# Query weights of a decode kernel: one load over 128 partitions, or four loads over strided partitions

## The chip, the cores and the metric

The kernel runs on one core of one Trainium2 chip. The metric is the device time in microseconds (us). Before the change it is 1275.88 us, the median of three runs (1275.86 to 1275.93). The core has TensorE (matrix products), VectorE, ScalarE and GpSimd, a sequencer called SyncE or SP that here only issues transfers, and 16 DMA engines that carry data between HBM and the on-chip memory SBUF, which has 128 partitions.

## The reference, cut to what matters

One token goes through a layer norm, and the result through an attention block with a long cache (16 query heads, 8 key/value heads, 65,536 positions of 256 values, bf16) and through a gated feed-forward block. The two are added to the input.

```python
B, Sq, D = 1, 1, 448
Hq, Hkv, Sk, Dh = 16, 8, 65536, 256
...
def _A_ref(x, k_cache, v_cache, wq, wo):
    ...
    q = (x @ wq).reshape(B, Sq, Hq, Dh).transpose(0, 2, 1, 3)
    scores = jnp.einsum("bhqd,bhkd->bhqk", q, k) * (Dh ** -0.5)
    p = _softmax(scores, axis=-1)
    o = jnp.einsum("bhqk,bhkd->bhqd", p, v)
    return o.transpose(0, 2, 1, 3).reshape(B, Sq, Hq * Dh) @ wo
...
x = A_x
xn = _layernorm(x, axis=-1)
return x + _A_ref(xn, A_k_cache, A_v_cache, A_wq, A_wo) + _B_ref(xn, B_w_r, B_w_gate, B_w_up, B_w_down)
```

The query weights `wq` are 448 x 4096 values, 3584 KB. The keys and the values are 256 MB each. Every byte is used once.

## The kernel before

**Tiling.** A key/value head's cache is cut into four units (`U` = 4): in each, every one of the 128 partitions holds 128 positions of 256 values (`SBN` = 128 positions, 64 KB for a partition, 8 MB for a unit). There are 32 units of K and 32 of V. They go through `ring`, an SBUF area of three slots (line 92): K units use slots 0 and 1 in turn, V units slot 2, and the last V units slots 0 and 1 too. Slot 2 first holds the query weights (`wq_area`, line 96: 14,336 values, 28 KB, in each partition) and small temporaries of the layer norm.

**Work on a unit.** TensorE transposes K in pieces of 128 x 128 (`k_T`), VectorE and ScalarE copy the transposed pieces to `kt_all`, TensorE multiplies them with the current queries (`k_QK`) and brings the scores back to 128 partitions (`k_JT`). After the four units of a head come the maximum, the exponentials and the products with V (`pe_V`). One turn (`turn_K`) works on K of unit u and V of unit u - 4.

**Queues.** The program is written as lists of entries, one list for each engine, with waits by name (`W`), operations (`O`) and transfers. `item` (line 243) puts a transfer on SP's list: first its waits, then for each part of the item a DMA start that adds 16 to the semaphore of the part when the part has landed. `items[key]` keeps the semaphore and the count that stand for "all parts landed", and `W_item` makes an engine wait for that count. SP works through its list strictly in order; `emit` writes out the entries, and every DMA is started at line 949. The list begins with `wq`, which waits for nothing, then the K units 0 to 3 (units 0 to 4 in two halves each, with semaphores of their own), V unit 0, then K and V in turn (lines 291 to 300). K unit u waits until TensorE has done with unit u - 2, V unit t until V unit t - 1 is done with, and V unit 0 until the queries exist. Two tiny loads (the input and a weight row) are issued by ScalarE's queue.

**Who uses wq.** `pe_setup` makes TensorE wait for it (`W_item("pe", "wq")`) ahead of `qrow`, 28 products that give the query row. VectorE scales the row, four small products transpose it, and the queries go to `qT_sb`. The semaphore `wq` is used once more at the end, for a part of the last V unit (`LAST_SEMS`, line 16); counts for that continue from the total so far (`semtot`).

`flat_src` (line 266) sees a weight matrix in HBM as 128 rows of equal length, one for each partition:

```python
def flat_src(src, n):
    return src.rearrange("a b -> (a b)").rearrange("(p n) -> p n", p=P)
```

## Time and profile before

| | |
|---|---|
| median of three runs | 1275.88 us |
| the profiled execution | 1275.78 us |
| its span in the trace | 1274.5 us |
| HBM read | 549.03 MB, 431 GB/s over the span |
| busy: TensorE / VectorE / ScalarE / GpSimd | 952.7 / 571.6 / 436.8 / 8.1 us |
| the transfer of wq | 3584 KB, 11.5 us from issue to landing |

The span is what the trace covers, from the first to the last recorded event of the execution; the device time holds about 1.3 us more. Times in the views below are microseconds from the start of the span. A packet is one row of a transfer on one DMA engine; packets of under 512 bytes are mostly the semaphore writes at the end of a transfer, one on each engine. In a window of the DMA view, a packet belongs to the window in which it starts and brings its whole time with it, so that a short window's share can exceed 100%. In the chain of waits, a DMA piece is one transfer from its issue to its landing, or the part of it that nothing else covers.

### The profile page before, as it was taken

What the parts mean: (1) busy time and instruction counts of PE and PEld (TensorE: products, weight loads), DVE (VectorE), ACT (ScalarE), POOL (GpSimd) and SP (SyncE); (2) the same over time, 40 slices, a digit from 0 to 9 for tenths busy, and PEclk for the clock granted to TensorE, in tenths of its full rate; (3) what the DMA queues carried; (4) which work ended last, traced back from release to release, by engine and by line L of the source; (5) the groups of instructions that cost most, each with busy time, mean ns of one, the idle gap of its engine ahead of it and who ended that gap; (6) DMA issues with size and microseconds to landing.
All of it is one profiled execution on the core that took longest, in us unless ns stands there. A gap on an engine that the chain in (4) does not pass through costs nothing.

```text
span 1274.5 us, 23452 instructions
## 1 busy us (share of the span) xinstructions
PE 952.7 (75%) x9685; PEld 620.7 (49%) x9685; DVE 571.6 (45%) x1083; ACT 436.8 (34%) x656; POOL 8.1 (1%) x38
## 2 busy tenths in 40 slices
PE   4998987768767778677678677687776787776664
PEld 2776655445544455454455444454444554444321
DVE  4665544445434355344454343453444544434310
ACT  1554433244323334233333242343333333323300
POOL 2000000000000000000000000000000000000000
PEclk8999998899888899888898888998888998888886
DMA  9999999999999999999999999999999999999998
GB/s 406 431 433 436 436 436 428 434 430 442 434 432 428 436 430 440 434 432 428 436 432 438 434 432 428 436 434 438 432 432 432 432 438 434 436 428 434 427 433 365
DMA packets 12356, 549.18 MB, mean 431 GB/s; under 512 B 1335, under 2 KB 1978, under 8 KB 2874
## 3 DMA queue, kind: packets, MB, share of 16 engines
q1 hardware_dynamic: 12340, 549.03, 99.8%
q8 instruction: 7, 0.11, 0.0%
q14 instruction: 3, 0.02, 0.0%
q10 hardware_dynamic: 6, 0.00, 0.0%
HBM read 549.03 MB, written 0.00 MB: 431 GB/s over the span
## 4 chain that ended last, share of the span: by engine, by line
DMA 78%; PE 18%; ACT 2%; issue 1%; DVE 1%; SPq 0%; ACTq 0%; DVEq 0%
DMA ring<-in_A_v_cache_dram 69%; PE ps_o L428 13%; DMA ring<-in_A_k_cache_dram 5%; PE ps_t L428 3%; DMA kt_all<-in_A_wo_dram 2%; DMA ring<-in_A_wo_dram 2%; PE ps_q L428 2%; ACT kt_all L492 2%; PE ps_m L428 1%; SPq L949 0%; DVE kt_all L490 0%; ACT S_sb L573 0%; PE ps_s L428 0%; DVE kt_all L731 0%; DVE kt_all L854 0%
## 5 line engine op out<-in xcount | busy, mean ns | idle before, releaser
L428 PE MATMUL ps_t<-ident_f,ring 128*128 128x128 f32 x4096 | 585.2, 285 | 81.3 <-DMA ring<-in_A_k_cache_dram 59.6
L490 DVE COPY kt_all<-ps_t 128x1024 bf16<-128x1024 bf16 x768 | 486.7, 684 | 289.1 <-PE ps_q L428 284.9
L428 PEld LDWEIGHTS ps_t<-ident_f,ring 128*128 128x128 f32 x4096 | 448.7, 143 | 233.6 <-issue 133.8
L492 ACT ACTIVATE kt_all<-ps_t 128x1024 bf16<-128x1024 bf16 x256 | 262.2, 1024 | 498.0 <-PE ps_q L428 497.9
L428 PE MATMUL ps_o<-ring,p_sb 128*4 128x512 bf16 x2040 | 177.9, 511 | 206.1 <-DMA ring<-in_A_v_cache_dram 201.7
L428 PEld LDWEIGHTS ps_o<-ring,p_sb 128*4 128x4 bf16 x2040 | 53.5, 102 | 294.6 <-issue 267.5
L428 PE MATMUL ps_q<-kt_all,q_cur 128*2 128x512 bf16 x2056 | 164.5, 397 | 0.3 <-DVE kt_all L490 0.3
L514 ACT ACTIVATE s<-ps_q 98x512 bf16<-98x512 f32 x257 | 151.8, 591 | 1.3 <-PE ps_q L428 1.3
L596 DVE RECIPROCAL rs<-ps_m 128x4 f32<-128x4 f32 x29 | 5.3, 182 | 275.1 <-PE ps_m L428 275.1
L583 ACT ACTIVATE p_sb<-S_sb 128x128 bf16<-128x128 bf16 x64 | 18.9, 307 | 265.4 <-PE ps_o L428 262.6
L428 PEld LDWEIGHTS ps_s<-sel_bf,s 128*128 128x128 bf16 x1032 | 64.3, 97 | 5.2 <-ACT s L514 1.9
L428 PE MATMUL ps_s<-sel_bf,s 128*128 128x8 bf16 x1032 | 63.4, 167 | 1.3 <-ACT s L514 1.3
L639 DVE CAST ob_sb<-ps_o 100x512 bf16<-100x512 f32 x29 | 20.1, 692 | 90.9 <-PE ps_o L428 90.9
L428 PEld LDWEIGHTS ps_q<-kt_all,q_cur 128*2 128x2 bf16 x2056 | 26.3, 79 | 44.9 <-issue 44.9
L428 PEld LDWEIGHTS ps_m<-rowsum,ones_f 128*128 128x128 f32 x58 | 12.3, 265 | 21.9 <-issue 21.9
L492 ACT ACT_TABLE_LOAD x7 | 9.0, 1283 | 27.0 <-PE ps_q L428 27.0
L543 DVE TENSOR_REDUCE m1p<-S_sb (+1 forms) x33 | 13.9, 421 | 4.4
L428 PE MATMUL ps_m<-rowsum,ones_f 128*128 128x4 f32 x58 | 14.8, 326 | 0.0
L541 DVE CAST S_sb<-ps_s 128x256 f32 (+1 forms) x33 | 13.6, 413 | 1.9 <-PE ps_s L428 1.9
L573 ACT ACTIVATE S_sb<-S_sb,negmax 128x512 bf16<-128x512 bf16 x16 | 13.2, 852 | 3.3 <-DVE negmax L567 3.3
L428 PE MATMUL ps_m<-diag,ones_f 2*128 2x2 f32 x58 | 11.2, 260 | 3.7 <-DVE diag L558 0.6
L428 PEld LDWEIGHTS ps_m<-diag,ones_f 2*128 2x128 f32 x58 | 8.7, 187 | 10.6 <-DVE diag L558 10.6
(97 smaller groups left out, 125.4 us busy)
## 6 DMA issues: line engine op xcount, KB each, us to landing
ring<-in_A_k_cache_dram SPq DMA_DIRECT2D x10, 4096.0 KB, 28.3
ring<-in_A_v_cache_dram SPq DMA_DIRECT2D x1, 4096.0 KB, 23.1
ring<-in_A_wq_dram SPq DMA_DIRECT2D x1, 3584.0 KB, 11.5
ring<-in_A_wo_dram SPq DMA_DIRECT2D x1, 2688.0 KB, 28.5
ring<-in_A_v_cache_dram SPq DMA_DIRECT2D x1, 2048.0 KB, 27.2
ring<-in_B_w_gate_dram SPq DMA_DIRECT2D x1, 1568.0 KB, 17.1
ring<-in_B_w_up_dram SPq DMA_DIRECT2D x1, 1568.0 KB, 20.5
ring<-in_B_w_down_dram SPq DMA_DIRECT2D x1, 1568.0 KB
```

The source lines that it names most:

```text
L428: return pe.matmul(*a, **k)
L490: O(e, ("EV", s, m), lambda it: nc.vector.tensor_copy(out=kt[:, :], in_=tb[:, :]), f"ev{m}")
L492: O(e, ("EV", s, m), lambda it: nc.scalar.activation(out=kt[:, :], in_=tb[:, :], func=ACTF.Copy), f"ev{m}")
L514: O("act", ("EVQ", s), lambda it: nc.scalar.activation(out=s2[s % 2][0:QROWS, :], in_=ps_q[0:QROWS, :], func=ACTF.Copy), "evq")
L541: O("dve", ("SCOPY", u), lambda it: nc.vector.tensor_copy(out=S_sb[:, at(it, SBN), :], in_=ps_sn), "sc")
L543: O("dve", ("SMAX", u), lambda it: nc.vector.tensor_reduce(out=m1p[:, :, at(it, 1)], in_=S_sb[:, at(it, SBN), :].rearrange("p n i -> p i n ...
L573: O("act", ("EXP", h, i), lambda it, i=i: nc.scalar.activation(out=S_sb[:, :, i], in_=S_sb[:, :, i], func=ACTF.Exp, bias=negmax[:, i:i + 1 ...
L583: O("act", ("PC", t, c), lambda it: nc.scalar.activation(out=p_sb[:, c, :, :], in_=S_sb[:, n:n + CH, :], func=ACTF.Copy), "pc")
L596: O("dve", ("RS", t), lambda it: nc.vector.reciprocal(out=rs[:, :, :], in_=ps_m[0:P, C_TOT:C_TOT + NH * rep]))
L639: O("dve", ("OB", t), lambda it: nc.vector.tensor_copy(out=ob_sb[0:OROWS, :], in_=ps_o[0:OROWS, :]))
```

## The change

The transfer of `wq`, one over partitions 0 to 127, becomes four, still on SP's queue and still first in it. Each takes every n-th partition from partition o on, and the same rows of the weights in HBM:

```diff
-    item("wq", [(wq_area, flat_src(A_wq, WQN), "wq")])
+    item("wq", [(wq_area[o:P:n, :], flat_src(A_wq, WQN)[o:P:n, :], "wq") for o, n in ((0, 8), (4, 8), (2, 4), (1, 2))])
     for u in range(U):
         k_item(u)
     v_item(0)
```

| transfer | partitions | rows |
|---|---|---|
| (0, 8) | 0, 8, 16, ... 120 | 16 |
| (4, 8) | 4, 12, 20, ... 124 | 16 |
| (2, 4) | 2, 6, 10, ... 126 | 32 |
| (1, 2) | 1, 3, 5, ... 127 | 64 |

Together they cover each partition once. Every row is 28 KB as before. The count that stands for "wq has landed" becomes 64 in place of 16. On the engines' lists nothing else differs: the other four are the same, and SP's has four wq transfers of 16, 16, 32 and 64 rows where it had one of 128.

## The prediction

> **What bounds the kernel now.** I read the profile in this order: the page for the bound, the chain of waits for what starts and ends the run, the DMA packets in short windows for the first load, and the timeline of TensorE for who waits for it.

> From the page, in its order: the span, the DMA engines' busy share and rate in forty slices, the SP queue's packets, megabytes and share of 16 engines, and the chain by engine.

> ```profile
> span 1274.5 us, 23452 instructions
> ...
> DMA  9999999999999999999999999999999999999998
> GB/s 406 431 433 436 436 436 428 434 430 442 434 432 428 436 430 440 434 432 428 436 432 438 434 432 428 436 434 438 432 432 432 432 438 434 436 428 434 427 433 365
> ...
> q1 hardware_dynamic: 12340, 549.03, 99.8%
> ...
> DMA 78%; PE 18%; ACT 2%; issue 1%; DVE 1%; SPq 0%; ACTq 0%; DVEq 0%
> ```

> The run is one stream of 549.03 MB, and its 16 DMA engines are busy 99.8% of the span. No slice has a hole. So a microsecond more of transfer at the front has no gap behind it in which to vanish, and a microsecond less is a microsecond won. The chain's first pieces (start, length, what) show where the front lies:

> ```profile
> 0.74 0.39 SPq L949
> 1.13 0.06 issue
> 1.19 20.78 DMA ring<-in_A_k_cache_dram
> 21.96 0.04 issue
> 22.01 1.97 PE ps_t L428 x8
> ```

> SP issues the query weights (wq) at 0.74 for 0.39 us, then the first half of K unit 0 at 1.19; that half lands at 21.97, behind wq on the same engines, and only then does TensorE start on K. TensorE's timeline (start, busy, line, output<-input, count, idle before) says that wq itself is not what it waits for longest:

> ```profile
> 14.00 3.16 PE L428 MATMUL ps_q<-ring,xnT_sb 128*2 128x512 bf16 x28 [0.51 <-DVE xnT_sb L414]
> 17.96 0.26 PE L428 MATMUL ps_m<-sel_bf,ring 98*128 98x8 bf16 x4 [0.80 <-DVE ring L416]
> 22.01 1.32 PE L428 MATMUL ps_t<-ident_f,ring 128*128 128x128 f32 x5 [3.79 <-DMA ring<-in_A_k_cache_dram]
> ```

> The query row starts when VectorE has the input ready, not on wq, and 3.79 us of idle time end with K. So wq counts here as bytes ahead of K in the stream, not as a value that is late.

> The rows of that stream one by one: packets on the SP queue, MB, and their time as a share of 16 engines, in the windows 1.5 to 2.0, 7 to 8, 11.0 to 11.5 and 12.0 to 12.5 us.

> ```profile
> q1 hardware_dynamic: 13, 0.37, 289.5%
> ...
> q1 hardware_dynamic: 15, 0.43, 100.0%
> ...
> q1 hardware_dynamic: 20, 0.33, 152.8%
> ...
> q1 hardware_dynamic: 12, 0.39, 181.9%
> ```

> The second line: 100% of 16 x 1 us over 15 packets is 1.067 us for one 28 KB row of wq, 26.9 GB/s for one engine. The fourth: 181.9% of 16 x 0.5 us over 12 is 1.213 us for a 32 KB row of K, 27.0 GB/s. The first line: 13 of the first 16 rows start within this window and take 289.5% of 8 us / 13 = 1.78 us each, 0.71 us above a later row: starting the stream costs that once. The third is the end of wq: 10 of its 20 packets are the 4-byte semaphore writes that end a transfer on each engine; 152.8% of 8 us less 10 K rows of 1.213 us leaves 0.1 us for the ten, 0.01 us each.

> **The change, part by part.** One transfer of 128 rows becomes four of 16, 16, 32 and 64: partitions 0, 8, 16 ..., then 4, 12, ..., then 2, 6, ..., then the odd ones. Bytes and row length (28 KB) stay, and if each transfer is dealt to all 16 engines, an engine still gets 1+1+2+4 = 8 rows.

> *Issue.* Three more instructions on SP, 0.39 us each plus 0.06 between: 3 x 0.45 = 1.35 us. Queued behind them on SP are K's four first halves (the first from 1.19 to 2.54) and everything later. This costs nothing because the engines have wq to move until 11 us, far past 2.54. Within wq, the second transfer is issued at 1.19 and, with the 1.01 us from issue to first packet that wq shows (0.74 to 1.75), ready at 2.2, while the first rows last until 1.75 + 1.78 = 3.5. Without that cover 1.35 us would be lost.

> *Start.* A 16-row transfer could be ready sooner than a 128-row one. The nearest row is the one-row load of x on the ACT queue: issued at 0.73, its packet lies in the window from 1.60, so 0.9 us against 1.01. Between 0 and 0.1 us gained; I take 0.

> *Semaphores.* TensorE now waits for four times 16 counts. Three more 0.01 us writes for each engine: 0.03 us. Query row and transposed queries (14.0 to 18.3) have 3.7 us before K lands; whatever delays wq delays K, behind it, by as much, so that slack stays.

> *The rows themselves.* This decides. Rows of 28, 32 and, in most of the run, 64 KB (549.03 MB in 99.8% of 16 x 1274.5 us is 27.0 GB/s) all go at 27 GB/s for an engine, whatever place in HBM they are read from. Common to these transfers is where they go: all 128 partitions, dealt out in one way. A fixed rate on a fixed division looks like a link of fixed width at the destination, sixteen of them with eight partitions each. The trace cannot show whether the limit is there or in the engine, since no large transfer in it covers fewer partitions. If it is in the engine, or if a link's eight partitions are neighbours, rows 8 apart fall on 16 links and the cost is 0. If they are grouped in another way, say twice four, partitions 0, 8, 16 ... meet two by two on half of the links: a row takes 2 x 1.067 us. The second transfer meets on the other half. In the third and fourth an engine that gets neighbouring rows has 8e+2, 8e+6, then 8e+1, 8e+3, 8e+5, 8e+7: all engines step through the same halves together, and every one of the eight rows is doubled: 8 x 1.067 = 8.5 us. Bounds: 0 and 8.5, and a gain at the start below. I take the upper end, since of the ways to group 128 partitions by eight, only those that part rows 8 apart leave this pattern alone, less 0.5 us: engines that start apart (13 rows begin over a quarter of a us, so two partners are about 0.1 us apart) run alone for that long after each of the five changes of half, 5 x 0.1.

> [...]

> *Sum.* 0 (issue) + 0 (start) + 0.03 + 8.0 = 8.0 us, passed whole to the end: the 25 us windows from 25 to 1175 us show the DMA engines 98 to 103% busy, and TensorE, 24 of 25 us busy from 25 to 100, starts later by the same amount. The profiled execution took 1275.78 us (span 1274.5, 1.3 around it), 0.1 below the median of 1275.88. Forecast: 1275.88 + 8.0 = 1283.9.

> **The rivals.**
> *Only the first two transfers collide.* If rows of the third and fourth are dealt so that the engines hold different links, as in a 128-row transfer, only two rows double: 2 x 1.067 = 2.1 us, 1278.0; with the third colliding too, four rows, 4.3 us, 1280.2. For it: the 128-row transfer evidently deals without collisions. Against: with 2 and 4 rows for an engine, neighbours are the simplest dealing.
> *Nothing collides (the other side: not slower).* The limit is in each engine. Then only the start moves. Gain: up to 0.1 us from the shorter first issue, and some of the spread with which the engines leave wq: its semaphore writes start over the two windows from 10.5 to 12.0, about 0.9 us, and the slowest sets the end. Time 1275.0 to 1276.0, at 1275.7. For it: a rate that is the same for every row length would also come from the engine. Against: nothing in the trace. It decides if the first 16 rows of the change take 1.8 us, not 2.8 or more.
> *The split does not spread.* If a 16-row transfer used fewer engines, wq would last longer than doubled: above 1285. The instruction's row count divides by 16 as 128 does, so I give this little.

> **How the numbers follow.** Every row doubled: 0.50, at 1283.9, its own range 1282.8 to 1285.0. Partly doubled: 0.20, 1277.5 to 1281, half of it above the bound. Nothing collides: 0.28. Fewer engines: 0.02. The bound of 0.2% is 2.55 us, about what a measurement of this kernel can tell. Slower by more: 0.50 + 0.10 + 0.02 = 0.62. Faster by more would take 2.55 us, and the whole time before the first packet is 1.75: 0.02, taken from the third case. Within: 0.10 + 0.26 = 0.36. The range reaches from the middle of the no-collision case to the top of the first, 1275.2 to 1285.0, leaving out under two in ten.

> **What would show it.** Right: wq's 28 KB packets at about 2.1 us each; its last semaphore writes near 20 us, not 11; the first K half landing near 30; K packets at 1.213 us as before; the slices after the first unchanged. Partly: two or four of each engine's eight packets long. Wrong: packets of 1.06 us throughout and K landing at 22. If K lands late and the end does not move, a gap that I did not see has taken the delay.

## The result and the profile after

The changed kernel takes 1277.81 us (median of 22 runs, 1277.69 to 1278.04), the kernel before in the same sessions 1275.97 us (22 runs, 1275.75 to 1276.23). That is 1.84 us more, a ratio of 1.0015 with a 95% interval of 1.0008 to 1.0021: slower, by less than the 0.2% that the chances went by, and less than a quarter of the 8.0 us forecast.

The page of the changed kernel, the same lines as before:

```profile
span 1276.5 us, 23455 instructions
...
DMA  9999999999999999999999999999999999999998
GB/s 378 426 448 421 442 429 433 439 437 429 427 435 433 444 429 427 435 427 448 431 427 431 431 442 435 429 429 433 439 437 429 429 433 437 439 429 429 429 433 365
...
q1 hardware_dynamic: 12388, 549.03, 99.7%
...
DMA 77%; PE 18%; ACT 2%; issue 1%; SPq 1%; DVE 1%; ACTq 0%; DVEq 0%
```

The bytes are the same, the packets are 48 more (three more semaphore writes on each of 16 engines), and the span is 2.0 us longer. The first slice is much poorer, 378 GB/s in place of 406: 28 GB/s over 31.9 us is 0.89 MB, and 0.89 MB at 433 GB/s is 2.1 us. Every other slice differs by at most 20 GB/s, some up and some down, so most of the loss lies in the first. The chain's first pieces:

```profile
0.73 0.62 SPq L949
1.36 0.06 issue
1.42 0.57 SPq L949
1.98 0.05 issue
2.03 0.58 SPq L949
2.62 0.04 issue
2.66 0.59 SPq L949
3.25 0.04 issue
3.29 20.27 DMA ring<-in_A_k_cache_dram
23.56 0.04 issue
23.61 1.97 PE ps_t L428 x8
```

K's first half is issued at 3.29 in place of 1.19 and lands at 23.56 in place of 21.97, 1.6 us later. The issue moved by 2.1 us and the landing by less, so the landing does not simply follow the issue. TensorE's timeline shows who waits:

```profile
13.98 3.15 PE L428 MATMUL ps_q<-ring,xnT_sb 128*2 128x512 bf16 x28 [0.51 <-DVE xnT_sb L414]
17.93 0.26 PE L428 MATMUL ps_m<-sel_bf,ring 98*128 98x8 bf16 x4 [0.80 <-DVE ring L416]
23.61 1.97 PE L428 MATMUL ps_t<-ident_f,ring 128*128 128x128 f32 x8 [5.42 <-DMA ring<-in_A_k_cache_dram]
```

The query row still starts at 14.0 and still behind VectorE: wq is not late for it. The wait for K grew from 3.79 to 5.42 us.

What happened to wq's rows is seen in the DMA packets. SP's queue in the windows 2.0 to 3.7, 3.7 to 4.7, 5.65 to 6.75 and 7.5 to 8.05 us, each of which holds the start of 16 rows (0.46 MB), an engine's first, second, third and fourth; the other packets are semaphore writes:

```profile
q1 hardware_dynamic: 18, 0.46, 113.1%
...
q1 hardware_dynamic: 30, 0.46, 200.7%
...
q1 hardware_dynamic: 32, 0.46, 141.8%
...
q1 hardware_dynamic: 16, 0.46, 193.6%
```

Share times 16 engines times the window, divided by 16 rows: 1.92, 2.01, 1.56 and 1.06 us for a row. The first three rows of each engine before the change, in the windows 1.7 to 2.5, 3.4 to 4.2 and 4.5 to 5.25 us:

```profile
q1 hardware_dynamic: 16, 0.46, 215.8%
...
q1 hardware_dynamic: 16, 0.46, 134.8%
...
q1 hardware_dynamic: 16, 0.46, 149.8%
```

That is 1.73, 1.08 and 1.12 us; the fourth row takes 1.06 us in the trace. Rows five to eight are at 1.06 to 1.07 us in both kernels. So the rows of the two 16-row transfers are slow, the row that follows them is half slow, and the rest of the 32- and 64-row transfers runs at the old rate. At the end of the run the last transfer lands at 1273.97, 2.05 us later than before in these two profiles. Of these, 0.2 us come from the profiled run of the kernel before, which lies that much below its median. The 0.2 to 0.3 us between K's 1.6 us and the 1.84 us of the medians were not located.

### The profile page after: what moved, and what is told of

It reads as the page before. It is cut to its first block, busy times and chain, and to the rows that moved or that the text cites. A ratio compares the mean times of both kernels' runs of the same rounds, so it can differ in the third digit from the quotient of the medians.

```text
span 1276.5 us, 23455 instructions
## 1 busy us (share of the span) xinstructions
PE 952.5 (75%) x9685; PEld 620.2 (49%) x9685; DVE 573.6 (45%) x1083; ACT 436.9 (34%) x656; POOL 8.0 (1%) x38
## 2 busy tenths in 40 slices
DMA  9999999999999999999999999999999999999998
## 3 DMA queue, kind: packets, MB, share of 16 engines
q1 hardware_dynamic: 12388, 549.03, 99.7%
HBM read 549.03 MB, written 0.00 MB: 430 GB/s over the span
## 4 chain that ended last, share of the span: by engine, by line
DMA 77%; PE 18%; ACT 2%; issue 1%; SPq 1%; DVE 1%; ACTq 0%; DVEq 0%
DMA ring<-in_A_v_cache_dram 68%; PE ps_o L428 13%; DMA ring<-in_A_k_cache_dram 5%; PE ps_t L428 3%; DMA kt_all<-in_A_wo_dram 2%; DMA ring<-in_A_wo_dram 2%; PE ps_q L428 2%; ACT kt_all L492 2%; PE ps_m L428 1%; SPq L949 1%; DVE kt_all L490 0%; ACT S_sb L573 0%; PE ps_s L428 0%; DVE kt_all L731 0%; DVE kt_all L854 0%
## 5 line engine op out<-in xcount | busy, mean ns | idle before, releaser
L428 PE MATMUL ps_t<-ident_f,ring 128*128 128x128 f32 x4096 | 583.9, 284 | 80.6 <-DMA ring<-in_A_k_cache_dram 56.3
L428 PEld LDWEIGHTS ps_t<-ident_f,ring 128*128 128x128 f32 x4096 | 447.9, 143 | 232.7 <-issue 136.4
L428 PE MATMUL ps_o<-ring,p_sb 128*4 128x512 bf16 x2040 | 178.8, 512 | 209.4 <-DMA ring<-in_A_v_cache_dram 205.0
L428 PEld LDWEIGHTS ps_o<-ring,p_sb 128*4 128x4 bf16 x2040 | 53.4, 102 | 298.0 <-issue 270.9
L428 PE MATMUL ps_q<-kt_all,q_cur 128*2 128x512 bf16 x2056 | 164.3, 396 | 0.3 <-DVE kt_all L490 0.3
L428 PEld LDWEIGHTS ps_s<-sel_bf,s 128*128 128x128 bf16 x1032 | 64.7, 98 | 5.3 <-ACT s L514 1.9
L428 PE MATMUL ps_s<-sel_bf,s 128*128 128x8 bf16 x1032 | 63.7, 167 | 1.3 <-ACT s L514 1.3
L428 PEld LDWEIGHTS ps_q<-kt_all,q_cur 128*2 128x2 bf16 x2056 | 26.3, 79 | 44.0 <-issue 44.0
L428 PEld LDWEIGHTS ps_m<-rowsum,ones_f 128*128 128x128 f32 x58 | 12.3, 264 | 22.8 <-issue 22.8
L428 PE MATMUL ps_m<-rowsum,ones_f 128*128 128x4 f32 x58 | 14.8, 326 | 0.0
L428 PE MATMUL ps_m<-diag,ones_f 2*128 2x2 f32 x58 | 11.2, 260 | 3.6 <-DVE diag L558 0.6
L428 PEld LDWEIGHTS ps_m<-diag,ones_f 2*128 2x128 f32 x58 | 8.7, 187 | 10.5 <-DVE diag L558 10.5
```

Of the source, the lines that this page charges most:

```text
L428: return pe.matmul(*a, **k)
```

## The experiments

Two theories were set against each other first. A: rows of a 16-row transfer meet two by two on links at the destination. B: every further transfer has a price, 1.84 / 3 = 0.61 us. Every kernel below is the kernel before with another line 291; times are medians, and the reference time is that of the kernel before in the same session (1275.85 to 1275.96 us). Where an edit shows a line that goes, it is the change's; `...` stands for the front of the line, which stays as in the change.

### Without 16-row transfers, three and four of them

```diff
-    ... for o, n in ((0, 8), (4, 8), (2, 4), (1, 2))])
+    ... for o, n in ((0, 4), (2, 4), (1, 2))])
```

> The two 16-row transfers (0, 8) and (4, 8) become one of 32 rows, (0, 4); the other two stay. Theory A, meeting rows: only rows of a 16-row transfer meet two by two at the destination and are slow, so here every 28 KB packet after an engine's first takes 1.06 to 1.08 us and what is left of the 1.84 us is at most the later start (0.5 us, first packet at 2.25 in place of 1.75): 1275.7 to 1276.5 us against 1275.97 before. Theory B, a price for each further transfer: 1.84 us for three is 0.61 us each, two are left: 1277.2 us.

```diff
-    ... for o, n in ((0, 8), (4, 8), (2, 4), (1, 2))])
+    ... for o, n in ((0, 4), (2, 4), (1, 4), (3, 4))])
```

> Four transfers of 32 rows each, every fourth partition from 0, 2, 1 and 3: as many transfers as in the change, none of 16 rows. Theory A, meeting rows: as with three transfers, 1275.7 to 1276.5 us, no packet after the first above 1.1 us. Theory B, a price for each further transfer: three further ones as in the change, 1277.8 us.

Measured: 1276.05 us with three transfers and 1276.08 us with four, beside 1275.91 before; both ratios 1.0001 (0.9992 to 1.001). In the window 4 to 8 us of the kernel with four transfers:

```profile
q1 hardware_dynamic: 87, 1.58, 93.1%
```

1.58 MB are 55 rows; 93.1% of 64 us over 55 is 1.08 us for a row. As many transfers as in the change, no row of doubled length, no loss that can be told (the interval ends at 1.3 us more, theory B asks for 1.84): theory B is out. The first packet starts at 2.08 us in both, 0.33 later than before, and the medians show 0.14 and 0.17 us of it. An engine's first row begins over a stretch of 0.7 us (1.75 to 2.46 before, 2.08 to 2.74 with three transfers), and at the end of wq the slowest engine is where it was: the last of K's 16 first rows starts at 11.77 before, at 11.76 with three transfers and at 11.72 with four.

### Only 16-row transfers, eight of them, and four

```diff
-    ... for o, n in ((0, 8), (4, 8), (2, 4), (1, 2))])
+    ... for o, n in ((0, 8), (4, 8), (2, 8), (6, 8), (1, 8), (5, 8), (3, 8), (7, 8))])
```

> Eight transfers of 16 rows, every eighth partition. Theory A, meeting rows: each of an engine's eight rows meets another; the two of the change cost 0.7 us each if the late start of 0.5 us is taken off 1.84, and 1.06 us each if rows are doubled in full: 1281.5 to 1284.9 us, with packets near 2 us all through. Theory B: seven further transfers at 0.61 us: 1280.3 us, and packets that are not longer in the later transfers.

Measured: 1283.77 us, 7.86 more than before, ratio 1.0061 (1.0046 to 1.0076). SP's queue in the window 8 to 12 us:

```profile
q1 hardware_dynamic: 60, 0.86, 97.3%
```

30 of the 60 packets are rows: 97.3% of 64 us over 30 is 2.08 us, semaphore writes included; the rows alone take 2.06 us in the trace, from the second of each engine to the eighth. That is what theory A expects.

```diff
-    ... for o, n in ((0, 8), (4, 8), (2, 4), (1, 2))])
+    ... for o, n in ((0, 8), (4, 8), (2, 8), (6, 8), (1, 2))])
```

> The change with its 32-row transfer cut into two of 16, partitions 2, 10, 18, ... and 6, 14, 22, ...: four of an engine's eight rows meet in place of two. Eight of them cost 7.9 us, 0.98 us each: four make 1275.97 + 3.9 = 1279.9 us, with four long rows and four of 1.06 us. If an engine got neighbouring rows of the 32-row transfer, as the prediction assumed, those two rows met already and nothing changes: 1277.8 us.

Measured: 1279.72 us, 3.87 more, ratio 1.0031 (1.0019 to 1.0042), as worked out beforehand. Windows 5.6 to 6.7, 7.65 to 8.75, 9.7 to 10.8 and 11.6 to 12.25, an engine's third to sixth row:

```profile
q1 hardware_dynamic: 32, 0.46, 186.2%
...
q1 hardware_dynamic: 32, 0.46, 187.2%
...
q1 hardware_dynamic: 32, 0.46, 148.0%
...
q1 hardware_dynamic: 16, 0.46, 163.8%
```

2.05, 2.06, 1.63 and 1.06 us. The third and fourth row go to partitions 8e+2 and 8e+6, as in the change; as one 32-row transfer they took 1.56 and 1.06 us in the change, and 1.08 us in the kernel of four 32-row transfers; as two of 16 rows they take 2.05 and 2.06. This is the run that bears on the step that failed (below). The extra time goes with the number of rows in 16-row transfers: none 0.14 to 0.17 us, two 1.84, four 3.87, eight 7.86, between 0.9 and 1.0 for each.

### Destination or source

Half of the partitions in each transfer, as neighbours or as even and odd:

```diff
+    item("wq", [(wq_area[o:o + 64, :], flat_src(A_wq, WQN)[o:o + 64, :], "wq") for o in range(0, P, 64)])
```

> Two transfers of 64 neighbouring rows, partitions 0 to 63 and 64 to 127. Theory A with links that belong to groups of partitions on one half of the memory: each transfer reaches only half of the links, every row is doubled, 8 x 1.06 = 8.5 us: 1283.5 to 1284.5 us. [...] Theory A with links of neighbouring partitions would have no meeting of more than two neighbours' shares either: also doubled. Theory B: one further transfer, 0.61 us: 1276.6 us.

```diff
+    item("wq", [(wq_area[o:P:n, :], flat_src(A_wq, WQN)[o:P:n, :], "wq") for o, n in ((0, 2), (1, 2))])
```

> Two transfers of 64 rows, the even and the odd partitions, the same rows of the weights for both sides. Meeting rows at the destination: none in the change's 64-row transfer, so none here: 1275.7 to 1276.3 us, packets of 1.06 us after the first. If 64 rows collide because a transfer covers half of the partitions, whichever they are: 1285 us as with the neighbouring halves.

and the same two destinations with the sources exchanged. In these two kernels the weights land on other partitions than in the reference, so that only their time says something:

```diff
+    item("wq", [(wq_area[o:P:2, :], flat_src(A_wq, WQN)[64 * o:64 * o + 64, :], "wq") for o in (0, 1)])
```

> Destination even partitions, then odd; source rows 0 to 63, then 64 to 127 (weights land on other partitions than the reference has them). If the destination makes rows slow: as the even and odd transfers, 1275.7 to 1276.3 us. If the place of the source rows in HBM does: as the neighbouring halves, 1285 us with packets of 2.0 to 2.25 us.

```diff
+    item("wq", [(wq_area[64 * o:64 * o + 64, :], flat_src(A_wq, WQN)[o:P:2, :], "wq") for o in (0, 1)])
```

> The other way round: destination partitions 0 to 63, then 64 to 127; source rows even, then odd (weights land on other partitions than the reference has them). If the destination makes rows slow: 1285 us, packets of 2.0 to 2.25 us. If the source does: 1275.7 to 1276.3 us.

| destination | source rows | time, us | ratio and interval |
|---|---|---|---|
| halves | halves | 1285.04 | 1.0072 (1.0056 to 1.0087) |
| halves | even, odd | 1285.39 | 1.0073 (1.0056 to 1.009) |
| even, odd | even, odd | 1276.02 | 1.0 (0.9991 to 1.001) |
| even, odd | halves | 1276.77 | 1.0006 (0.9997 to 1.0016) |

The packets of the two exchanged kernels: destination halves in the window 13 to 17 us, then destination even and odd in the window 6 to 10 us.

```profile
q1 hardware_dynamic: 30, 0.86, 105.1%
```

```profile
q1 hardware_dynamic: 74, 1.66, 96.5%
```

105.1% of 64 us over 30 rows is 2.24 us; 96.5% of 64 us over 58 rows (16 of the 74 are semaphore writes) is 1.06 us. So with 64-row transfers the destination partitions make the rows slow, and the place of the source rows in HBM does not. For 16-row transfers the sources were not exchanged. The last kernel is 0.8 us above the kernel before with rows of 1.06 us: its engines start further apart (an engine's second row begins between 3.57 and 4.75, before between 3.44 and 4.16), and the last one leaves wq 0.5 us later. That is above what was expected, and its interval still includes no change.

### How rows are grouped

```diff
+    item("wq", [(wq_area[o:o + 16, :], flat_src(A_wq, WQN)[o:o + 16, :], "wq") for o in range(0, P, 16)])
```

> Eight transfers of 16 neighbouring partitions. Every eighth partition gave 2.06 us for a row, two rows on a link. If links belong to four neighbours (and four others far away), 16 neighbours meet four by four: 4.1 us for a row, 8 x (4.1 - 1.06) = 24.4 us more, 1300 us. If a link takes two at most, or the loss comes from a transfer having only 16 rows: 2.06 us and 1283.8 us as with every eighth.

Measured: 1297.76 us, 21.8 more, ratio 1.0171 (1.0154 to 1.0188). SP's queue in the window 10 to 30 us:

```profile
q1 hardware_dynamic: 160, 2.29, 96.9%
```

80 rows in 96.9% of 320 us are 3.88 us, and 3.84 without the semaphore writes. 16 rows every eighth partition take 2.06 us, 16 neighbours 3.84, which is 3.6 times a free row. The first expectation, neighbours that meet four by four, is the nearer one, though it had 4.1 us and 1300 us. So having 16 rows is not by itself what sets a transfer's rate, and if it is a shared link that makes rows slow, more than two can meet on one. That the links belong to groups of four neighbours is a reading of the 3.84 us, which no trace shows; other group sizes were not tried.

### The order reversed

```diff
-    ... for o, n in ((0, 8), (4, 8), (2, 4), (1, 2))])
+    ... for o, n in ((1, 2), (2, 4), (4, 8), (0, 8))])
```

> The change's four transfers in the opposite order: 64, 32, 16 and 16 rows. If two meeting rows cost what they cost wherever they stand: the same as the change, 1277.6 to 1278.0 us, with the long packets as an engine's seventh and eighth, and K's first rows up to twice as long as the eighth row's writes end. If the loss belongs to small transfers at the very start of the stream: 1275.9 to 1276.3 us.

Measured: 1278.71 us, 2.86 more than before (1275.85), ratio 1.0022 (1.0013 to 1.0031). Neither expected time holds, though the long packets are where the first expectation put them: the loss does not belong to the start of the stream, but at the end of wq the two rows cost 1.0 us more than at its head. Windows 9.2 to 9.8, 10.8 to 11.95 and 12.8 to 14.1: an engine's seventh and eighth row and its first row of K.

```profile
q1 hardware_dynamic: 32, 0.46, 310.8%
...
q1 hardware_dynamic: 32, 0.46, 178.6%
...
q1 hardware_dynamic: 32, 0.52, 136.3%
```

1.87, 2.05 and 1.77 us, against 1.06, 1.06 and 1.21 (a row of K) in a free stream: 0.80 + 0.99 + 0.56 = 2.35 us more. In the change it is 1.92 - 1.73, 2.01 - 1.08 and 1.56 - 1.12, so 0.19 + 0.93 + 0.44 = 1.56 us. At the head the first row is slow with or without a partner (1.73 us before the change), and meeting adds only 0.19 us to it. This accounts for 0.8 of the 1.0 us; where the rest comes from was not settled.

## Why the prediction was right and wrong

**The stream passes a delay to the end: right.** From nothing to 21.8 us, what wq lost came out as time, to within a few tenths of a us. K's first half moved by 1.6 us in the changed kernel and the end by 1.84.

**Issue: hidden as predicted, its size wrong.** K's first issue moved by 2.1 us, not 1.35, since the four instructions took 0.57 to 0.62 us each, not 0.39. With four transfers of 32 rows K is issued as late (3.47) and the time stays.

**Start: wrong in sign, of little weight.** The first packet came 0.4 us later (2.14 against 1.75), where 0 to 0.1 us earlier was allowed for. The splits without meeting rows start nearly as late (2.08); three of them end 0.06 to 0.17 us above the kernel before, and the one with exchanged sources 0.8 us above it. More transfers are not the reason: with eight blocks of 16 neighbours the first issue takes 0.39 us and the first packet comes at 1.77, as before the change, while strided partitions take 0.56 to 0.63 us and 2.08 to 2.14, and halves of 64 neighbours 0.57 us and 2.11. Why is open.

**The rows: the destination right, the count wrong.** The partitions that a transfer goes to set the time of a row (2.24 us with halves, 1.06 with even and odd). The step that failed is "In the third and fourth an engine that gets neighbouring rows has 8e+2, 8e+6, then 8e+1, 8e+3, 8e+5, 8e+7: all engines step through the same halves together, and every one of the eight rows is doubled". Two of eight were. The same partitions 8e+2 and 8e+6 meet as two transfers of 16 rows and not as one of 32, so, on the reading by links, a 32- or 64-row transfer (1.08 and 1.06 us for a row) must be dealt so that the engines stay on different links, as in a transfer of 128. This is inferred from the times of the rows: the trace does not name an engine's partitions, so which dealing that is stays open. The prediction had this as its first rival, two rows doubled, 1278.0 us against 1277.81 measured, gave it 0.20 together with the case of four doubled rows, and put it behind because "neighbours are the simplest dealing", which no row of the trace spoke for; the 128-row transfer, whose rows take 1.06 us and so do not meet, spoke against it. That a link's eight partitions are parted "say twice four" was the prediction's estimate, which no row before the change could test; the runs showed 2.06 us for a row where the partitions of a 16-row transfer lie 8 apart, and 3.84 us where they are neighbours. That the rival comes so near in number is partly luck: it adds 1.07 us for each of two rows, and the runs show 0.19 for the first, 0.93 for the second and 0.44 for the row behind them.

**The price of a row: nearly right.** 2 x 1.067 = 2.13 us was put down and 2.06 measured. Eight met rows cost 7.86 us, where the sum for eight was 8.0. But the 0.5 us that the sum took off for engines that start apart is not seen: in the kernel of eight 16-row transfers an engine's third row begins between 5.73 and 6.65 us, and every such row still takes 2.06 us.

**The sign that was to tell the cases apart was a bad one.** "It decides if the first 16 rows of the change take 1.8 us, not 2.8 or more": they took 1.92 although they met, and 1.89 in the kernel whose eight rows all meet. At the head of the stream the second row (2.01 against 1.08) decides.

**Splitting as such: no gain.** None of the splits was faster than the one transfer over 128 partitions. The split by even and odd partitions costs nothing that can be told (1276.02 us against 1275.96), the one by halves 9.1 us (1285.04 against 1275.91).

## What to carry to other kernels

In this kernel, whose DMA engines are busy 99.8% of the span, the first load counted by the time its rows occupied the engines, although nobody waited for its data. Look for that wherever the engines have no gaps. In a load that is split over partitions, look at which partitions each part goes to: here even and odd, or every fourth partition with 32 rows, left a row at 1.06 to 1.08 us; every eighth made it 2.06, halves 2.24 and blocks of 16 neighbours 3.84. Look at the time of single packets: in the changed kernel rows of 2.01 us in place of 1.08 showed the loss, where the DMA engines' busy share still reads 99.7%.
